# The first chunk's output projection turned round: weights standing, tokens moving

## The chip, the cores and the metric

The kernel runs on one core of one Trainium2 chip. The metric is the device time of one execution in microseconds (us). The kernel before took 358.76 us, the median of three runs (358.68 to 359.31 us).

## The reference

An attention-like scan is computed first; its result, laid out as 3072 tokens of 256 features, then goes through a gated feed-forward layer:

```python
def _attn_ref(x, a, B, C):            # x (4, 8, 768, 32); a (4, 8, 768); B, C (4, 8, 768, 16)
    log_a = np.log(np.clip(a, 1e-06, 1.0))
    for c in range(seq // 32):        # per batch and head
        cum = np.cumsum(la, axis=-1)
        L = np.exp(cum[:, :, :, None] - cum[:, :, None, :]) * causal
        y_intra = einsum('bhij,bhjd->bhid', einsum('bhin,bhjn->bhij', Cc, Bc) * L, xc)
        y_inter = einsum('bhin,bhnd->bhid', Cc, state) * exp(cum)[:, :, :, None]
        state = exp(sum(la)) * state + sum(Bx, axis=2)
    ...
def _moe_ref(x, w_gate, w_val, w_out):   # x (3072, 256); w (256, 1536), (256, 1536), (1536, 256)
    gate = 1.0 / (1.0 + np.exp(-(x @ w_gate)))
    val = x @ w_val
    return (gate * val @ w_out).astype(np.float32)
```

Everything is float32. The output is 3072 rows of 256 floats, 1 KB a row.

## The kernel before, in words

**Tiles and chunks.** The 768 positions of the sequence are cut into six chunks of 128. One chunk holds 128 positions of each of the four batches, so 512 tokens. For each chunk the scan gives the tokens' features, and then the feed-forward layer runs over twelve blocks `f` of 128 hidden features: TensorE (PE) makes a block's gate `pg` and value `pv` (128 features by 512 tokens, one PSUM bank each), ScalarE (ACT) takes the sigmoid of `pg` into `g`, and VectorE (DVE) multiplies it with `pv`, which gives the block `h`. When all twelve `h` of a chunk are there, the output projection `po` sums them against `w_out`.

**Two forms of a product.** Chunk 0's early products are plain float32 on whole weights (tiles `wr`, also `whole` in the code); a float32 matmul shows as two records on PE. Later products are made of a rounded high part and a low part in the type fp32r, three matmuls for one product (tiles `w`, `xh`, `xl`). All of chunk 0's `h` are single float32 tiles, and chunk 0's output projection is in plain float32 too.

**Two forms of the output projection.** `proj` (from L1190 in the code before, used by chunks 0 and 5) keeps 128 tokens of `h` standing in PE and moves 256 columns of the output weights: a tile of 128 tokens by 256 outputs for each batch. In chunk 0 that makes four accumulators of half a bank, 12 matmuls each (line L1214), a copy by ACT or DVE into a tile `o` (L1238) and one store of 128 rows of 1 KB (L1253). `proj_turned` (L1160 to L1192, used by chunks 1 to 4) keeps 128 columns of the weights standing and moves all 512 tokens of `h`: two accumulators of 128 outputs by 512 tokens, filled in turn by rounds of four blocks (L1176). DVE then turns them in squares of 32 by 32 (STREAM_TRANSPOSE, L1182) into a tile `o`, and 16 stores (L1189) each write 32 partitions, 32 KB, in pieces of 64 floats, 256 bytes.

**Order of the work.** The program is written out by a planner, `run()` (L194 to L283). Each piece of work is a task whose steps name an engine, a cost, what they need and what they make, and the buffers they take or give back. Among the steps that can begin, the planner takes the first by its model, with the lower due time first; a table `DUES` overrides due times by task name. What the planner writes is the fixed order of each engine's queue, and all five run in order. Three PSUM banks (`ps_mm`) go round between `pg`, `pv` and `po`; a bank comes free when ACT or DVE has read it. The scan's small matmuls (tiles `pcb`, `banks`, `local`) have banks of their own and stand on PE between the large ones, in insertions of about 16 to 64 small matmuls. They use decays that come by DMA from a DRAM tile `a_z` into six `ab` buffers (L341), are multiplied up by a scan on DVE (L484) and masked (L550, L686). All loads and stores after the start are issued by the queue SP in its own order: `tn`, `bn`, `xn`, `pp`, `ab` are inputs of the scan. Tiles of the tag `ut` (two buffers) hold the scan's result `y` of a pair of batches (L797) before it is split into `xh` and `xl`.

Of the kernel before, what the change touches and what calls it, by code (L numbers as in the profile page):

```python
# [15 lines left out]
DRAM = bass.MemoryType.DRAM  # L16

DUES = {
# [17 lines left out]
}  # L36
WARM = 3

# [35 lines left out]
def tile_ssd_then_gated_ffn(  # L74
# [11 lines left out]
    nc = tc.nc  # L86
# [574 lines left out]
    def faded(out, before, by, added, j):  # L661

        nc.vector.scalar_tensor_tensor(
            out=out[:, j], in0=before[:, j], scalar=by, in1=added[:, j], op0=ALU.mult, op1=ALU.add
        )
# [58 lines left out]
    class Pair:  # L724
# [44 lines left out]
        def after(self):  # L769

            p = self.p
            yield step("dve", 0.29, [("py", p)])
            pp = got["pp", p]
            local = [x.rearrange("p (j d) -> p j d", j=2) for x in fixed["local"]]
            ml = wk.tile([P, 2, NG * D], F32, tag="ml", name=f"ml{self.nm}")
            chosen(ml, local[0], 2)
            self.s1 = state_of(p, "sm")
            for j in range(2):
                yield step("dve", 0.42, [("pS", p - 2), ("ppp", p), ("pinter", p - 2)], [("pfirst", p)] if j else [], port=True)
                faded(self.s1, states2[p - 2], pp[:, j, L2 - 1 : L2], ml, j)  # L780
            if not self.more:
                return
            yield step("dve", 0.29, [], [("pafter", p)])
            mr = wk.tile([P, 2, NG * D], F32, tag="mr", name=f"mr{self.nm}")
            chosen(mr, local[1], 2)
            states2[p] = state_of(p, "sn")
            for j in range(2):
                yield step("dve", 0.42, [], [("pS", p)] if j else [], port=True)
                faded(states2[p], self.s1, pp[:, j, L - 1 : L], mr, j)

        def inner(self):

            p = self.p
            needs = [("whole", i) for i in range(NW)] if p == FIRST_P else [("plo", p - 2)]
            yield step("act", ACT_MM, [("py", p)] + needs, [("inner", p)])
            self.y = wk.tile([P, 2, NK, 2, L2], F32, tag="ut", name=f"y{self.nm}")
            nc.scalar.copy(self.y.rearrange("p i k u l -> p (i k) (u l)"), fixed["banks"][:, :, 2 * L : 3 * L])  # L797
# [242 lines left out]
    def halved(k, f):  # L1040
        return k == 0 and f < NHALF
# [113 lines left out]
    gs = {}  # L1155

    def turned(k):
        return 0 < k < NCH - 1

    outs = {}  # L1160

    def proj_turned(k, mt):

        ms = slice(mt * P, (mt + 1) * P)
        for n in range(0, NF, 4):
            some = range(n, n + 4)
            needs = [("h", k, f) for f in some] + sorted({("w", NF + f // 2) for f in some}) + ([] if n else [("gv", k)])
            yield step(
                "pe", 4 * 3 * 0.227, needs, [("proj", k)] if mt and n + 4 == NF else [], port=24, banks=int(n == 0)
            )  # L1170
            if n == 0:
                acc = ps_mm.tile([P, 512], F32, tag="mm", name=f"po{k}_{mt}")
            for f in some:
                w = wo[f // 2][:, f % 2, :, ms]
                for i, (part, of_h) in enumerate(((0, 0), (0, 1), (1, 0))):
                    nc.tensor.matmul(  # L1176
                        acc, w[:, part], hs[k, f][:, of_h], start=(f == 0 and i == 0), stop=(f == NF - 1 and i == 2)
                    )
        yield step("dve", 1.15, [("out", k - 2)], [("out", k, mt)], port=True, banks=-1)
        if mt == 0:  # L1180
            outs[k] = hp.tile([P, NB * RUN, 2 * 32], F32, tag=f"r{k % 2}", name=f"o{k}")
        nc.vector.transpose(outs[k].rearrange("p b (m t) -> p t b m", t=2)[:, mt], acc.rearrange("p (b r) -> p b r", r=32))  # L1182
        if mt == 0:
            return
        yield step("sp", 0.52 * 16, [("out", k, 0)], [("out", k)], 1.6)
        for b in range(NB):
            rows = out[b * S + k * L : b * S + (k + 1) * L].rearrange("(t r) m -> r t m", r=32)
            for q in range(NQ):
                nc.sync.dma_start(  # L1189
                    rows[:, :, 64 * q : 64 * q + 64], outs[k][32 * q : 32 * q + 32, RUN * b : RUN * b + RUN]  # L1190
                )

    def proj(k, j):
# [166 lines left out]
    def initial():  # L1360
# [2 lines left out]
        made = [(k, u) for k in keys for u in range(-6, 0)]  # L1363
        made += [(k, p) for k in ("plo", "pafter", "inner", "added") for p in range(2, FIRST_P)] + [("block", -1)]
        made += [("used", i) for i in (-2, -1)] + [(k, u) for k in ("cd", "inter") for u in range(2)]
        made += [("gv", -2), ("gv", -1), ("proj", -1), ("out", -1), ("out", 0)]
        yield step("none", 0.0, [], made)
        yield step("none", 4.9, [], [("a0",)])
        yield step("none", 0.6, [], [("bc", 0), ("bc", 1)])
# [145 lines left out]
```

## Time and profile before

The profiled execution took 358.8 us by its own time; its span, from the first to the last instruction, is 357.0 us.

| What | Before |
|---|---|
| Median of 3 runs | 358.76 us |
| Profiled execution: own time, span | 358.8 us, 357.0 us |
| PE busy | 349.7 us (98%), 3244 instructions |
| DVE, ACT, POOL busy | 164.0 us (46%), 148.3 us (42%), 167.8 us (47%) |
| Chunk 0's output matmuls (L1214) | 96 records |
| Granted PE clock | 1.00 in every stretch |

A row of a timeline reads: start in us, length in us, engine, line, operation, output <- inputs, shapes, number of instructions in the row, and in brackets what the engine waited for before it. The ends of matmuls are modelled and overlap, so the time that a stream of them takes is read from one start to the next. Group rows read: line, engine, operation, shapes, count | busy us, mean ns of one | idle before, and what ended it. SPq is the issuing of DMAs by the queue SP.

### The profile page before, as it was taken

What the parts mean: (1) busy time and instruction counts of PE and PEld (TensorE: products, weight loads), DVE (VectorE), ACT (ScalarE), POOL (GpSimd) and SP (SyncE); (2) the same over time, 40 slices, a digit from 0 to 9 for tenths busy, and PEclk for the clock granted to TensorE, in tenths of its full rate; (3) what the DMA queues carried; (4) which work ended last, traced back from release to release, by engine and by line L of the source; (5) the groups of instructions that cost most, each with busy time, mean ns of one, the idle gap of its engine ahead of it and who ended that gap; (6) DMA issues with size and microseconds to landing.
All of it is one profiled execution on the core that took longest, in us unless ns stands there. A gap on an engine that the chain in (4) does not pass through costs nothing.

```text
span 357.0 us, 7917 instructions
## 1 busy us (share of the span) xinstructions
PE 349.7 (98%) x3244; PEld 278.3 (78%) x3244; DVE 164.0 (46%) x287; ACT 148.3 (42%) x282; POOL 167.8 (47%) x171
## 2 busy tenths in 40 slices
PE   8989899999999999999999999999999999999996
PEld 3568378787788888888888888887888888888885
DVE  5879479877546684754650224530222210222201
ACT  2565984425885421355440244440044420344400
POOL 5536768666788635155460146562045520244400
PEclk9999999999999999999999999999999999999999
DMA  7989983515654345326320112000020000200000
GB/s 172 218 249 218 271 271 123 113 42 94 133 111 107 77 97 118 55 58 120 77 39 9 36 24 34 17 2 2 15 44 1 2 0 0 46 15 0 2 29 29
DMA packets 88949, 27.41 MB, mean 77 GB/s; under 512 B 78002, under 2 KB 81650, under 8 KB 88914
## 3 DMA queue, kind: packets, MB, share of 16 engines
q1 hardware_dynamic: 84754, 26.52, 31.6%
q10 hardware_dynamic: 4160, 0.39, 0.9%
q8 instruction: 25, 0.41, 0.5%
q14 instruction: 10, 0.08, 0.1%
HBM read 23.46 MB, written 3.44 MB: 75 GB/s over the span
## 4 chain that ended last, share of the span: by engine, by line
PE 88%; DMA 2%; ACT 2%; DVE 1%; SPq 1%; issue 0%
PE pg L1151 26%; PE pv L1151 25%; PE po L1176 18%; PE po L1214 6%; PE po L1225 2%; DMA wr<-in_moe_w_val_dram 2%; PE banks L693 2%; PE banks L677 1%; PE po L1226 1%; PE banks L719 1%; PE po L1222 1%; SPq L366 1%; PE pv L1142 1%; DVE wr L382 1%; PE local L700 0%; ACT wr L398 0%
## 5 line engine op out<-in xcount | busy, mean ns | idle before, releaser
L1119 POOL TENSOR_TENSOR h<-g,h 128x512 fp32r<-128x512 f32 x60 | 79.5, 1324 | 117.6 <-ACT h L1117 117.6
L1151 PE MATMUL pg<-xh,w 128*128 128x512 f32 x264 | 93.3, 394 | 0.0
L1151 PE MATMUL pv<-xh,w 128*128 128x512 f32 x264 | 92.2, 390 | 0.0
L1113 DVE TENSOR_TENSOR g<-pv,g 128x512 f32<-128x512 f32 x60 | 41.4, 691 | 91.1 <-PE pv L1151 89.6
L1117 ACT CAST h<-g 128x512 fp32r<-128x512 f32 x60 | 37.2, 620 | 73.1 <-DVE g L1113 73.1
L1176 PE MATMUL po<-h,w 128*128 128x512 f32 x288 | 66.7, 390 | 0.0
L1092 ACT ACTIVATE g<-pg 128x512 f32<-128x512 f32 x68 | 40.6, 597 | 55.9 <-PE pg L1151 55.2
L1176 PEld LDWEIGHTS po<-h,w 128*128 128x128 f32 x288 | 53.8, 188 | 11.3
L1151 PEld LDWEIGHTS pg<-xh,w 128*128 128x128 f32 x264 | 49.6, 188 | 11.1 <-issue 0.2
L1151 PEld LDWEIGHTS pv<-xh,w 128*128 128x128 f32 x264 | 49.6, 188 | 10.5 <-issue 0.2
L1151 PE MATMUL pg<-xl,w 128*128 128x512 f32 x132 | 51.4, 390 | 0.0
L1151 PE MATMUL pv<-xl,w 128*128 128x512 f32 x132 | 51.4, 389 | 0.0
L419 POOL TENSOR_TENSOR w<-wr,w 128x512 fp32r<-128x512 f32 x18 | 26.4, 1468 | 9.0 <-ACT w L417 9.0
L484 DVE TENSOR_TENSOR_SCAN ab<-ab,delta 128x512 f32<-128x512 f32 x20 | 28.5, 1437 | 1.6 <-DMA ab<-a_z 1.6
L1151 PEld LDWEIGHTS pg<-xl,w 128*128 128x128 f32 x132 | 24.8, 188 | 5.1 <-issue 0.2
L1151 PEld LDWEIGHTS pv<-xl,w 128*128 128x128 f32 x132 | 24.8, 188 | 5.1
L400 POOL TENSOR_TENSOR wr<-wr 128x512 int32<-128x512 int32 x18 | 21.9, 1224 | 13.5 <-ACT wr L398 7.4
L1182 DVE STREAM_TRANSPOSE o<-po 128x512 f32<-128x512 f32 x8 | 5.7, 717 | 41.8 <-PE po L1176 41.8
L1214 PE MATMUL po<-wr,h 128*128 128x256 f32 x96 | 23.2, 393 | 0.0
L1214 PEld LDWEIGHTS po<-wr,h 128*128 128x128 f32 x96 | 17.6, 188 | 3.8 <-issue 0.2
L820 POOL TENSOR_TENSOR xl<-y,xh 128x256 fp32r<-128x256 f32 x16 | 12.4, 775 | 10.8 <-ACT xh L818 10.6
L392 ACT ACTIVATE wt<-wr 128x512 f32<-128x512 f32 x18 | 12.0, 680 | 7.8 <-DVE wr L382 4.4
(145 smaller groups left out, 381.4 us busy)
## 6 DMA issues: line engine op xcount, KB each, us to landing
ab<-a_z SPq DMA_DIRECT2D x40, 128.0 KB
wr<-in_moe_w_gate_dram SPq DMA_DIRECT2D x6, 512.0 KB
wr<-in_moe_w_val_dram SPq DMA_DIRECT2D x6, 512.0 KB
wr<-in_moe_w_out_dram SPq DMA_DIRECT2D x6, 512.0 KB
xn<-in_x_dram SPq DMA_DIRECT2D x10, 256.0 KB
out_dram<-o SPq DMA_DIRECT2D x64, 32.0 KB
bn<-in_B_dram SPq DMA_DIRECT2D x10, 128.0 KB
tn<-in_B_dram SPq DMA_DIRECT2D x32, 32.0 KB
```

What stands on the lines that cost most here:

```text
L392: nc.scalar.activation(t, hw.bitcast(F32), AF.Prelu, scale=2.0**-112, alpha=2.0**32)
L400: nc.gpsimd.tensor_tensor(out=lw.bitcast(I32), in0=hw.bitcast(I32), in1=lw.bitcast(I32), op=ALU.add)
L419: engines[eng].tensor_tensor(out=lo, in0=lw, in1=hi.bitcast(F32), op=ALU.subtract)
L484: nc.vector.tensor_tensor_scan(out=t.rearrange("p h l -> p (h l)"), data0=t.rearrange("p h l -> p (h l)"), data1=delta.rearrange("p h l -> ...
L820: engines[eng].tensor_tensor(out=lo, in0=y, in1=hi.bitcast(F32), op=ALU.subtract)
L1092: nc.scalar.activation(gs[k, f], pm, AF.Sigmoid)
L1113: nc.vector.tensor_tensor(out=g, in0=pm, in1=g, op=ALU.mult)
L1117: copies[eng](hh, g)
L1119: engines[eng].tensor_tensor(out=hl, in0=g, in1=hh.bitcast(F32), op=ALU.subtract)
L1151: nc.tensor.matmul(pm, w[:, part, kt, fs], xx[:, kt], start=(i == 0), stop=(i == 3 * NK - 1))
L1176: nc.tensor.matmul(acc, w[:, part], hs[k, f][:, of_h], start=(f == 0 and i == 0), stop=(f == NF - 1 and i == 2))
L1214: nc.tensor.matmul(acc[:, :DM], hs[k, f][:, js], whole[NF + f // 2][:, f % 2], start=start, stop=stop, skip_group_check=True,)
```

## The change

Chunk 0's output takes the form of chunks 1 to 4. `turned(k)` is now true for chunk 0 as well, and `proj_turned` has a branch for single float32 blocks: a slice of the whole weights (every second column, 128 of them) stands, and the block's 512 tokens move. There are 24 matmuls of 128x512 (48 records) in place of 48 of 128x256 (96 records), and two accumulators in place of four. DVE turns each accumulator in two halves, into two tiles `o` of the tag `ut`, and SP issues 16 stores in 256 byte pieces in place of four stores of whole rows. Of the first pair of the scan in chunk 1, the step `inner`, which writes `y` into a `ut` tile, now needs chunk 0's output to be stored. The table `DUES` is replaced by another, which gives all engines a partly new order.

```diff
 DUES = {
-    "r": -31, "w6": -30, "w9": -25, "w11": 13, "w12": 14, "w13": 15, "w14": 16, "w15": 12.7, "w16": -2.4, "w17":
+    "r": -31, "w6": -30, "w9": -25, "w11": 8.5, "w12": 14.4, "w13": 269.7, "w14": 261.1, "w15": -0.5, "w16": -4,
...
         def inner(self):
             p = self.p
-            needs = [("whole", i) for i in range(NW)] if p == FIRST_P else [("plo", p - 2)]
+            needs = [("out", 0)] if p < FIRST_P + 2 else [("plo", p - 2)]
             yield step("act", ACT_MM, [("py", p)] + needs, [("inner", p)])
...
     def turned(k):
-        return 0 < k < NCH - 1
+        return k < NCH - 1
...
     def proj_turned(k, mt):
...
             for f in some:
+                if single(k, f):
+                    w = whole[NF + f // 2][:, f % 2].rearrange("p (m t) -> p t m", t=2)[:, mt]
+                    nc.tensor.matmul(acc, w, hs[k, f], start=(f == 0), stop=(f == NF - 1))
+                    continue
...
         yield step("dve", 1.15, [("out", k - 2)], [("out", k, mt)], port=True, banks=-1)
-        if mt == 0:
-            outs[k] = hp.tile([P, NB * RUN, 2 * 32], F32, tag=f"r{k % 2}", name=f"o{k}")
-        nc.vector.transpose(outs[k].rearrange("p b (m t) -> p t b m", t=2)[:, mt], acc.rearrange("p (b r) -> p b r", r=32))
+        n = 1 if k else 2
+        if mt == 0 and k:
+            outs[k] = [hp.tile([P, NB * RUN, 2 * 32], F32, tag=f"r{k % 2}", name=f"o{k}")]
+        elif mt == 0:
+            outs[k] = [wk.tile([P, NB * RUN // 2, 2 * 32], F32, tag="ut", name=f"o{k}_{i}") for i in range(2)]
+        for i in range(n):
+            nc.vector.transpose(
+                outs[k][i].rearrange("p b (m t) -> p t b m", t=2)[:, mt],
+                acc.rearrange("p (i b r) -> p i b r", i=n, r=32)[:, i],
+            )
         if mt == 0:
             return
         yield step("sp", 0.52 * 16, [("out", k, 0)], [("out", k)], 1.6)
...
                 nc.sync.dma_start(
-                    rows[:, :, 64 * q : 64 * q + 64], outs[k][32 * q : 32 * q + 32, RUN * b : RUN * b + RUN]
+                    rows[:, :, 64 * q : 64 * q + 64], outs[k][b * n // NB][32 * q : 32 * q + 32, at : at + RUN]
                 )
```

**On PE, the end of chunk 0's products.** `pv_11` is the last value block; `m`, `bd` and `xn` belong to an insertion of the scan of chunk 1, `cd`, `sn`, `sm` to the next. Before:

```order
L1151 MATMUL pv_11_803<-xh_425,w_738 128x512
L1214 MATMUL po_0_832<-wr_538,h_0_315 128x256
L1214 MATMUL po_0_832<-wr_538,h_1_354 128x256
L1214 MATMUL po_0_832<-wr_551,h_2_506 128x256
L1214 MATMUL po_0_832<-wr_551,h_3_540 128x256
L567 MATMUL pcb_1_687<-m_0_824,xn_0_297 32x64 x16
L578 MATMUL pcb_1_687<-xn_0_297,bd_0_839 32x64 x8
L567 MATMUL pcb_1_687<-m_1_830,xn_0_297 32x64 x16
L578 MATMUL pcb_1_687<-xn_0_297,bd_1_828 32x64 x8
L1214 MATMUL po_1_904<-wr_538,h_0_315 128x256
```

And now:

```order
L1152 MATMUL pv_11_804<-xh_425,w_735 128x512
L569 MATMUL pcb_1_628<-m_0_788,xn_0_297 32x64 x16
L580 MATMUL pcb_1_628<-xn_0_297,bd_0_829 32x64 x8
L569 MATMUL pcb_1_628<-m_1_826,xn_0_297 32x64 x16
L580 MATMUL pcb_1_628<-xn_0_297,bd_1_824 32x64 x8
L1179 MATMUL po_0_889<-h_0_315,wr_537 128x512
L1179 MATMUL po_0_889<-h_1_354,wr_537 128x512
L1179 MATMUL po_0_889<-h_2_505,wr_582 128x512
L1179 MATMUL po_0_889<-h_3_520,wr_582 128x512
L624 MATMUL pcb_1_628<-cd_833,sn_476 64x64 x4
```

The insertion stands directly behind the last value block instead of behind the first four output matmuls, and each output matmul moves 512 columns. Elsewhere on PE the insertions of the scan of chunks 2 and on stand behind other blocks than before; from the start of chunk 0's last products there are 17 insertions in both orders, with the same small matmuls.

**On DVE, at the end of chunk 0.** `o_0` and `o_1` are the two halves of the turned output, `g_0` is the first product of chunk 1's blocks, `m_0` and `m_1` are masks that the scan's insertion in chunk 1 needs. Now:

```order
L615 SCALAR_TENSOR_TENSOR sm_1068<-sn_512,pp_1_797,ml_2_1066 128x64
L1193 STREAM_TRANSPOSE o_0_1105<-po_0_889 128x256
L1193 STREAM_TRANSPOSE o_1_1106<-po_0_889 128x256
L641 TENSOR_TENSOR xl_937<-pcb_957,xh_936 128x2x2x64 x2
L588 TENSOR_TENSOR mr_2_1126<-pcb_957,mask 128x128
L518 SCALAR_TENSOR_TENSOR sn_1132<-sm_1068,pp_1_797,mr_2_1126 128x64
L688 TENSOR_TENSOR m_0_1164<-banks,ab_0_801 128x512
L1193 STREAM_TRANSPOSE o_0_1105<-po_1_930 128x256
L1193 STREAM_TRANSPOSE o_1_1106<-po_1_930 128x256
L688 TENSOR_TENSOR m_1_1180<-banks,ab_1_899 128x512
L1114 TENSOR_TENSOR g_0_1177<-pv_0_1170,g_0_1177 128x512
```

Before, no instruction on DVE read `po` of chunk 0; ACT copied the accumulators. The four transposes are new, two ahead of `xl` and two between `m_0` and `m_1`.

**On SP, at the start of chunk 1.** Now all 16 stores of chunk 0 stand in one piece ahead of the loads `pp_0`, `bn_1`, `ab_1`, `pp_1`, `tn_0` and `ab_2` (of the eight rows of `tn_0` two are shown):

```order
L343 DMA ab_0_1134<-a_z 64x512 x2
L308 DMA bn_0_1162<-in_B_dram 128x16x16
L1204 DMA out_dram<-o_0_1105 32x4x64 x8
L1204 DMA out_dram<-o_1_1106 32x4x64 x8
L354 DMA pp_0_1275<-a_q 128x1x128 x2
L308 DMA bn_1_1288<-in_B_dram 128x16x16
L343 DMA ab_1_1291<-a_z 64x512 x2
L354 DMA pp_1_1317<-a_q 128x1x128 x2
L321 DMA tn_0_1331<-in_B_dram 32x4x64
L321 DMA tn_0_1331<-in_C_dram 32x4x64
...
L343 DMA ab_2_1433<-a_z 64x512 x2
```

Before, the stores of the four batches stood in two pairs, the second of them here:

```order
L341 DMA ab_0_1201<-a_z 64x512 x2
L1253 DMA out_dram<-o_2_1084 128x256
L1253 DMA out_dram<-o_3_1155 128x256
L352 DMA pp_0_1227<-a_q 128x1x128 x2
L319 DMA tn_0_1245<-in_B_dram 32x4x64
L319 DMA tn_0_1245<-in_C_dram 32x4x64
```

So 16 store issues now stand where two stood. On DVE the scan of `ab_2` stands between the products `g_6` and `g_7` of chunk 1, and it waits for that load.

More of the change, by code (lines that the diff above doesn't have):

```diff
@@ L772, in after @@
             yield step("dve", 0.29, [("py", p)])
-            pp = got["pp", p]
             local = [x.rearrange("p (j d) -> p j d", j=2) for x in fixed["local"]]
@@ L779, in after @@
                 yield step("dve", 0.42, [("pS", p - 2), ("ppp", p), ("pinter", p - 2)], [("pfirst", p)] if j else [], port=True)
-                faded(self.s1, states2[p - 2], pp[:, j, L2 - 1 : L2], ml, j)
+                faded(self.s1, states2[p - 2], got["pp", p][:, j, L2 - 1 : L2], ml, j)
             if not self.more:
@@ L788, in after @@
                 yield step("dve", 0.42, [], [("pS", p)] if j else [], port=True)
-                faded(states2[p], self.s1, pp[:, j, L - 1 : L], mr, j)
+                faded(states2[p], self.s1, got["pp", p][:, j, L - 1 : L], mr, j)
         def inner(self):
             p = self.p
-            needs = [("whole", i) for i in range(NW)] if p == FIRST_P else [("plo", p - 2)]
+            needs = [("out", 0)] if p < FIRST_P + 2 else [("plo", p - 2)]
             yield step("act", ACT_MM, [("py", p)] + needs, [("inner", p)])
@@ L1166, in proj_turned @@
             some = range(n, n + 4)
-            needs = [("h", k, f) for f in some] + sorted({("w", NF + f // 2) for f in some}) + ([] if n else [("gv", k)])
+            needs = [n for f in some for n in ([("h", k, f, i) for i in range(2)] if halved(k, f) else [("h", k, f)])]
+            needs += sorted({("whole" if single(k, f) else "w", NF + f // 2) for f in some}) + ([] if n else [("gv", k)])
             yield step(
-                "pe", 4 * 3 * 0.227, needs, [("proj", k)] if mt and n + 4 == NF else [], port=24, banks=int(n == 0)
+                "pe", sum(0.88 if single(k, f) else 0.681 for f in some), needs,
+                [("proj", k)] if mt and n + 4 == NF else [], port=24, banks=int(n == 0)
             )
@@ L1188, in proj_turned @@
             for q in range(NQ):
+                at = RUN * (b % (NB // n))
                 nc.sync.dma_start(
-                    rows[:, :, 64 * q : 64 * q + 64], outs[k][32 * q : 32 * q + 32, RUN * b : RUN * b + RUN]
+                    rows[:, :, 64 * q : 64 * q + 64], outs[k][b * n // NB][32 * q : 32 * q + 32, at : at + RUN]
                 )
@@ L1365, in initial @@
         made += [("used", i) for i in (-2, -1)] + [(k, u) for k in ("cd", "inter") for u in range(2)]
-        made += [("gv", -2), ("gv", -1), ("proj", -1), ("out", -1), ("out", 0)]
+        made += [("gv", -2), ("gv", -1), ("proj", -1), ("out", -2), ("out", -1)]
         yield step("none", 0.0, [], made)
```

34 rows, old and new, of the table DUES are left out of this document.

## The prediction

> **What bounds the kernel now.** I read the page first: busy shares and the chain that ended last.
>
> ```profile
> PE 349.7 (98%) x3244; PEld 278.3 (78%) x3244; DVE 164.0 (46%) x287; ACT 148.3 (42%) x282; POOL 167.8 (47%) x171
> PE 88%; DMA 2%; ACT 2%; DVE 1%; SPq 1%; issue 0%
> ```
>
> TensorE is busy 98% of the span, and 88% of the chain is its own work. Shares are means, so I cut the span at the edges of the stages in the view of busy time by windows (length, then busy us and count of PE, PEld, DVE, ACT, POOL, then the clock, DMA share, GB/s):
>
> ```profile
> 0.00:42.20 42.20, 38.02 (x398) 23.41 (x398) 29.43 (x61) 24.68 (x53) 21.72 (x35) 1.00 0.90 218
> 42.20:61.50 19.30, 19.28 (x111) 14.96 (x112) 15.57 (x20) 13.94 (x28) 14.69 (x14) 1.00 0.68 219
> 61.50:89.03 27.53, 27.53 (x417) 21.51 (x415) 21.34 (x33) 11.92 (x30) 18.36 (x22) 1.00 0.41 86
> 89.03:353.90 264.87, 264.87 (x2328) 218.40 (x2320) 97.18 (x173) 97.74 (x172) 113.01 (x103) 1.00 0.21 43
> 353.90:357.00 3.10, 0.05 (x1) 0.00 (x0) 0.42 (x1) 0.00 (x0) 0.00 (x0) 1.00 0.25 85
> ```
>
> The granted clock is full throughout. In the first 42.2 us loads matter (DMA engines 90% busy) and PE waits 4 us. From 42.2 to 353.9 its busy time is the length of the window, so it never waits; 3.1 us of last stores follow. Chunk 0's output stands in the third window. Three things can move the time: the start of PE's closed stretch, the sum of PE's work in it, or a new wait that opens it. A gain on any other engine is worth nothing there.
>
> **The start.** Up to 42 us the queues of all engines stand as before, but for two value blocks and a gate block exchanged on PE and one small DVE step; the chain into the value block that ends the waiting is unchanged. I take zero, with 0.3 us either way: half of the last wait before it.
>
> ```profile
> 42.22 1.99 PE L1142 MATMUL pv<-xw,wr 128*128 128x512 f32 x4 [0.61 <-ACT g L1092]
> ```
>
> **PE's work removed.** The stream of the old output matmuls, from PE's timeline and from its group:
>
> ```profile
> 67.13 3.89 PE L1214 MATMUL po<-wr,h 128*128 128x256 f32 x16
> 71.58 7.52 PE L1214 MATMUL po<-wr,h 128*128 128x256 f32 x32
> L1214 PE MATMUL po<-wr,h 128*128 128x256 f32 x96 | 23.2, 393 | 0.0
> L1214 PEld LDWEIGHTS po<-wr,h 128*128 128x128 f32 x96 | 17.6, 188 | 3.8 <-issue 0.2
> ```
>
> Sixteen more records take 7.52 - 3.89 = 3.63 us, 0.227 us a record (the 393 ns of the group is a pipelined length and overlaps the next). 96 x 0.227 = 21.8 us go.
>
> **PE's work added.** 48 records of 512 columns in float32. The same shape, type and 128x128 weights stand in the trace at the early gates and values:
>
> ```profile
> 34.65 1.88 PE L1142 MATMUL pg<-xw,wr 128*128 128x512 f32 x4
> 38.08 1.88 PE L1142 MATMUL pg<-xw,wr 128*128 128x512 f32 x4
> 26.56 1.03 PE L1048 MATMUL pg<-xw,wr 128*128 128x256 f32 x4
> 27.42 1.03 PE L1048 MATMUL pv<-xw,wr 128*128 128x256 f32 x4
> L1142 PEld LDWEIGHTS pg<-xw,wr 128*128 128x128 f32 x8 | 1.6, 196 | 1.4 <-issue 1.4
> ```
>
> Between the two rows at 34.65 and 38.08 stands one more of four, so eight records take 3.43 us, 0.429 each: 48 x 0.429 = 20.6 us, a gain of 1.2 us. Where does it come from? Columns are the same in number. At 256 columns L1048 took 0.86 us for four, 0.215 a record, half of 0.429; L1214 took 0.227 at the same size and type. So the old output matmuls carry about 12 ns a record that the early ones do not. One difference in the code is the moving operand: L1214 moves whole weights with every second word left out, L1048 and L1142 move contiguous tokens. The new matmul moves a contiguous `h`; its strided operand is the weights, as at L1142, whose loads took 196 ns for 188 and hide under 429.
>
> Bounds. If the 12 ns belong to every record of this stage, whatever moves, the new one takes 0.441 and the gain is 21.8 - 21.2 = 0.6 us. If time goes by columns at the old rate, 2 x 0.227 = 0.454 and the gain is zero. Above that no row points: a load would have to last over twice its 196 ns to show. I take 0.429, since this is the nearest row in shape, type and operands, and keep 0 to 1.2.
>
> The page "TensorE: Matmul & The Clock Gate" of the Trainium skill (section "Back-to-back issue gap") gives the isolated gap as columns by 2.4 GHz plus 2.5 ns, which says that halving the count of matmuls saves 2.5 ns each. An estimate from it is 48 x 2.5 = 0.12 us, no gain that can be seen. The early rows (215 and 429 ns, against its estimates of 216 and 429 for two columns' cycles each) agree; the 227 of L1214 does not.
>
> **Insertions.** Both orders hold 17 insertions of the scan between large matmuls in the closed stretch, with the same small matmuls, so I cost their moves at nothing on PE. What makes their inputs is hidden beside PE, with margins: the first, now directly behind `pv_11`, needs two masks.
>
> ```profile
> 59.83 0.67 DVE L550 TENSOR_TENSOR m<-pcb,ab 128x512 f32<-128x512 f32 x1
> 61.01 0.68 DVE L550 TENSOR_TENSOR m<-pcb,ab 128x512 f32<-128x512 f32 x1
> 61.50 1.97 PE L1214 MATMUL po<-wr,h 128*128 128x256 f32 x8
> ```
>
> The second ended at 61.69 before, and is now one product earlier in DVE's queue. `pv_11` ends at 61.5 and the second mask's matmuls come some 0.4 us later. If that cover is gone, PE waits 0.3 us or less.
>
> **ACT, DVE.** ACT loses four copies of 366 ns, which PE never waited for. DVE gains four transposes of 128x256:
>
> ```profile
> L1238 ACT COPY o<-po 128x256 f32<-128x256 f32 x4 | 1.5, 366 | 8.3 <-PE po L1214 8.3
> L1182 DVE STREAM_TRANSPOSE o<-po 128x512 f32<-128x512 f32 x8 | 5.7, 717 | 41.8 <-PE po L1176 41.8
> L811 DVE TENSOR_TENSOR y<-banks,y 128x256 f32<-128x256 f32 x8 | 3.4, 423 | 10.3 <-ACT y L797 4.5 <-PE local L719 4.3 <-PE banks L700 1.5
> 89.21 1.29 DVE L686 TENSOR_TENSOR m<-banks,ab 128x512 f32<-128x512 f32 x2 [0.87 <-PE banks L677]
> ```
>
> Half of 717 ns is 359, another PSUM read of that size took 423; I take 0.42, 1.7 us in all, between 1.4 and 2.9 (each as dear as a whole one). DVE is 21.3 of 27.5 us busy there. Behind the last two wait `m_1` and `g_0`: `po` ends about 87.1 (the insertion behind it takes 0.7), `m_0` begins 0.2 behind the insertion, 0.65 of the two in the last row, and is done at 88.7, so the transposes end at 89.6, and `m_1` and `g_0` at about 91.0; its bank is wanted by the third block after it, past 92. Cost nothing; at the upper price half a microsecond.
>
> **SP.** Sixteen store issues replace four and now stand ahead of loads that chunk 1 needs. The rows that price them:
>
> ```profile
> 146.11 9.98 SPq L1189 DMA_DIRECT2D out_dram<-o  x16
> 200.05 7.57 SPq L1189 DMA_DIRECT2D out_dram<-o  x16
> 93.98 0.40 SPq L319 DMA_DIRECT2D tn<-in_B_dram  x1
> 98.18 0.43 SPq L319 DMA_DIRECT2D tn<-in_C_dram  x1
> 98.66 1.21 SPq L352 DMA_DIRECT2D pp<-a_q  x2
> 99.92 2.00 SPq L341 DMA_DIRECT2D ab<-a_z  x2
> 102.03 0.53 SPq L306 DMA_DIRECT2D bn<-in_B_dram  x1
> 163.76 1.12 SPq L341 DMA_DIRECT2D ab<-a_z  x2
> 167.85 1.23 DVE L484 TENSOR_TENSOR_SCAN ab<-ab,delta 128x512 f32<-128x512 f32 x1 [0.19 <-DMA ab<-a_z]
> L1113 DVE TENSOR_TENSOR g<-pv,g 128x512 f32<-128x512 f32 x60 | 41.4, 691 | 91.1 <-PE pv L1151 89.6
> 116.59 0.28 DVE L663 SCALAR_TENSOR_TENSOR sm<-sq,pp,ml 128x64 f32<-128x64 f32 x1
> 58.77 0.39 PE L1151 MATMUL pg<-xh,w 128*128 128x512 f32 x1
> 60.13 0.39 PE L1151 MATMUL pv<-xh,w 128*128 128x512 f32 x1
> 94.74 0.69 PE L677 MATMUL banks<-bct 32*64 32x128 f32 x32
> 96.54 0.50 PE L1151 MATMUL pg<-xh,w 128*128 128x512 f32 x1
> ```
>
> The stores can begin at 89.6 and take 7.6 to 10.0 us of issuing: until 97.2 to 99.6. Then `pp_0` 1.2, `bn_1` 0.5, `ab_1` 1.1 to 2.0, `pp_1` 1.2, eight of `tn_0` 4.6, `ab_2` 1.1 to 2.0, and about 0.1 between them, 0.5: the issue of `ab_2` ends at 107.4 to 111.6. An `ab` was there 2.97 us after its issue ended (164.88 to 167.85): 110.4 to 114.6. The scan (1.23), a small step (0.28) and `g_7` (0.69) follow on DVE, which gives back a bank at 112.6 to 116.8. PE wants it for `pg_9`. Its start: `pg_0` at 87.9 (89.03 less the 1.2), 18 blocks of 1.36 (58.77 to 60.13), and one insertion of 2.0 (94.74 to 96.54, and the slower first record after it): 114.4. So at the fast end there is a margin of 1.8 us, at the slow end a wait of 2.4. I take the fast end, no wait: the rows of 0.43 us are the many, the slow ones single. `ab_1`, due before `g_5`, comes by the same sum 3 us after 100.3 to 103.6; its scan, a small step, a mask and `g_5` then end at 106.2 to 109.5, for a bank that `pg_7` wants at 109.0 (14 blocks and the insertion): it binds less.
>
> **The sum.** The profiled execution took 358.8 us, 357.0 of span and 1.8 around it; its time and the median of the runs (358.76) are one. 358.8 - 1.2 = 357.6 us.
>
> **The rivals.** A measurement of this kernel can tell about 0.2%, 0.7 us, from no change: under 358.04 is faster, over 359.48 slower.
>
> *The extra 12 ns stay.* For it: the fp32r records (58.77 to 60.13 is six) also start every 0.227 us, 12 ns over half of 0.429, though they move no strided operand. Against: L1142 and L1048. Then 358.8 - 0.6 = 358.2. Chance 0.14.
>
> *Columns alone count*, 0.454 a record: 358.8. Against it stands L1214 beside L1048: the excess was not there at the same columns. Chance 0.07. The rule of the Trainium skill's page "TensorE: Matmul & The Clock Gate" comes out beside it: 358.8 less the estimate of 0.12 is 358.7.
>
> *SP's stores delay `ab_2`.* One mechanism: sixteen issues hold back six groups of loads, DVE stands in its scan of `ab_2`, `g_7` behind it keeps a bank, PE stops ahead of `pg_9`. It decides from 1.8 us of delay over the fast sum, so from stores that take 9.4 us with all else fast. Up to a wait of 1.9 us the gain is only eaten: 357.6 to 359.5, chance 0.15. At the slow end, 357.6 + 2.4 = 360.0, slower; so too if the stores take 12 us with fast loads (4.4 us late, 2.6 of wait: 360.2). For it: one of two rows has 9.98. Against: in that stretch the 0.43 us issues are the many and the long ones single. Chance 0.15.
>
> *Another wait from the new order* that eats the gain, in chunks 2 to 5, where all insertions have moved: 0.04, with the time at 358.8.
>
> **How the numbers follow.** The forecast, 357.6, has 0.45; with the start's 0.3 either way it stretches from 357.2 to 357.9. Faster: 0.45 and a small part, 0.05, of the mild delay and the staying 12 ns: 0.50. Slower: 0.15. Same: 0.35. The range leaves out the dear end of the SP case and a gain beyond 1.7: 357.1 to 359.5, which takes in both ends of the matmul's price and a wait of up to 1.9 us.
>
> **What would show it.** Right: 48 records at the new line, four of them every 1.72 us in a stretch without insertions; `pg_0` of chunk 1 starting near 87.9; busy time equal to length from 42.2 to about 352.7; no wait in front of `pg_9`; the issue of 16 stores under 9 us. The first rival shows as 1.76 us for four, the second as 1.82. The SP case shows as idle PE near 114, released by DVE's `g`, with DVE released by the DMA of `ab`. I am wrong beyond size if PE's first closed stretch begins elsewhere than at 42.2, or if PE's idle time after it is over 1 us.

## The result

The changed kernel takes 362.41 us, the median of six runs (361.45 to 365.08). The kernel before, timed beside it, takes 358.84 us (358.41 to 359.31). The ratio is 1.0116, with an interval of 1.0087 to 1.0144: slower by 1.2%, where a gain of 1.2 us was forecast. The time lies outside the predicted range.

The profiled execution took 361.84 us by its own time, with a span of 360.0, so it stands 0.6 us under the median. From the page of the changed kernel, busy shares and the chain that ended last:

```profile
span 360.0 us, 7831 instructions
PE 350.4 (97%) x3196; PEld 275.3 (76%) x3196; DVE 165.0 (46%) x291; ACT 146.5 (41%) x281; POOL 165.8 (46%) x168
PE 85%; DMA 3%; DVE 3%; issue 3%; ACT 3%; SPq 2%; DVEq 0%; ACTq 0%
```

PE has 48 records fewer and yet is busy 0.7 us longer, and "issue" went from 0% to 3% of the chain. The windows cut at the same stages as in the prediction (columns as there):

```profile
0.00:41.88 41.88, 37.87 (x399) 23.45 (x399) 28.41 (x61) 24.68 (x53) 22.03 (x35) 1.00 0.92 209
41.88:61.59 19.71, 19.71 (x111) 14.69 (x111) 14.76 (x20) 13.91 (x28) 13.94 (x13) 1.00 0.72 236
61.59:88.53 26.94, 26.94 (x369) 18.51 (x368) 18.12 (x32) 10.90 (x25) 16.25 (x18) 1.00 0.46 91
88.53:356.70 268.17, 265.86 (x2328) 218.64 (x2320) 103.30 (x177) 96.99 (x176) 113.55 (x104) 1.00 0.21 42
356.70:360.00 3.30, 0.00 (x1) 0.00 (x0) 0.42 (x1) 0.00 (x0) 0.00 (x0) 1.00 0.23 79
```

The third window, in which chunk 0's output stands, is shorter by 0.6 us (26.94 for 27.53). The fourth is longer by 3.3 (268.17 for 264.87): same number of PE records, but 2.3 us in which PE is idle, where it had no idle time at all. The tail, from PE's last record to the end of the span, is 0.25 longer (3.28 for 3.03; the last window before still holds 0.05 us of PE's work). What PE waited for from 42.5 us on, in the view of waits (total, times, longest):

```profile
PE banks L702 <- issue: 2.0, 2, 1.8
PE pv L1143 <- ACT g L1093: 0.6, 1, 0.6
PE pg L1152 <- DVE g L1114: 0.3, 1, 0.3
```

The middle row was there before. The last is the wait ahead of `pg_9` that the prediction's SP rival named. The first is the large one, and its releaser is "issue": PE waited for nothing that the profile shows. Its two places in PE's timeline:

```profile
134.23 0.22 PE L702 MATMUL banks<-xn,bd 64*32 64x64 f32 x1
136.28 0.30 PE L702 MATMUL banks<-xn,bd 64*32 64x64 f32 x2 [1.83 <-issue]
136.51 0.50 PE L1183 MATMUL po<-h,w 128*128 128x512 f32 x1
...
184.26 0.34 PE L702 MATMUL local<-xn,bd 64*32 64x64 f32 x6
184.77 0.25 PE L702 MATMUL banks<-xn,bd 64*32 64x64 f32 x2 [0.16 <-issue]
```

At 134.23 PE stops with two small matmuls (four instructions with their loads) of an insertion still to do, and goes on 2.05 us later. Their operands had long been there, since others of the same line had just used them, and neither the load nor the matmul at which PE goes on has a semaphore to wait for. A later insertion stops in the same way at 184.5.

**What they share.** The page's table of DMA queues has, in both kernels, a queue that brings instructions:

```profile
q8 instruction: 25, 0.41, 0.5%
```

25 transfers make 0.41 MB, 16 KB each. I numbered PE's instructions in the trace, loads, matmuls and the few others, from the start. There are 6429 of them, so 257 to a transfer. Both stops stand in front of a number that leaves 193 when divided by 256 (3009 and 4289). The count can be had from windows that end at the two stops (the bracket behind PE and the one behind PEld):

```profile
0.00:135.50 135.50, 130.12 (x1490) 93.55 (x1490) 92.94 (x158) 75.56 (x153) 86.17 (x94) 1.00 0.64 151
135.50:184.60 49.10, 48.32 (x638) 39.44 (x639) 31.03 (x56) 19.13 (x37) 23.15 (x25) 1.00 0.44 85
```

638 + 639 and 3 other instructions of PE that these columns leave out make 1280, five times 256, between the two stops. So a block edge of PE's code stands there. PE passes such edges all the time without a trace; these two have in common that another edge stands in the same insertion, 256 instructions ahead. An insertion with all its parts holds 320 instructions (160 small matmuls with their loads, more than the 16 to 64 named in the description of the kernel) and takes 2.26 us, about 7 ns each, while large matmuls take 113 ns an instruction (0.227 us for a load and a matmul). In an insertion with two edges PE uses up a whole block in under 2 us. In the changed kernel the edges moved, since 96 instructions were gone ahead of them and the insertions stand behind other blocks. In the kernel before, one insertion after 42 us holds two edges as well, the one at 150.70 us (at its 10th and 266th instruction), and PE passes both without a stop. So two edges in one insertion are not the whole condition; experiment 2 takes this up.

The sum of the difference in span, 3.0 us: pauses 2.28 + 0.39 (the insertions took 4.54 and 2.65 us for 2.26), the wait ahead of `pg_9` 0.48 (its idle time and a slower entry), other small differences in chunks 1 to 4 0.1, tail 0.25, chunk 0's output -0.6, and up to it +0.1 net (start 0.34 earlier, the stretch to 61.59 0.43 longer, for which I have no cause).

### The profile page after: what moved, and what is told of

The parts are those of the page before. It is cut to its first block, busy times and chain, and to the rows that moved or that the text cites. A ratio compares the mean times of both kernels' runs of the same rounds, so it can differ in the third digit from the quotient of the medians.

```text
span 360.0 us, 7831 instructions
## 1 busy us (share of the span) xinstructions
PE 350.4 (97%) x3196; PEld 275.3 (76%) x3196; DVE 165.0 (46%) x291; ACT 146.5 (41%) x281; POOL 165.8 (46%) x168
## 4 chain that ended last, share of the span: by engine, by line
PE 85%; DMA 3%; DVE 3%; issue 3%; ACT 3%; SPq 2%; DVEq 0%; ACTq 0%
PE pg L1152 22%; PE pv L1152 22%; PE po L1183 18%; PE po L1179 6%; PE po L1240 2%; DMA wr<-in_moe_w_val_dram 2%; PE banks L695 1%; PE warm L135 1%; PE banks L679 1%; PE po L1241 1%; DMA ab<-a_z 1%; SPq L321 1%; PE pg L1049 1%; PE banks L721 1%; DVE ab L486 1%
## 5 line engine op out<-in xcount | busy, mean ns | idle before, releaser
L486 DVE TENSOR_TENSOR_SCAN ab<-ab,delta 128x512 f32<-128x512 f32 x20 | 29.3, 1474 | 2.5 <-DMA ab<-a_z 1.6
L1193 DVE STREAM_TRANSPOSE o<-po 128x512 f32<-128x512 f32 (+1 forms) x12 | 7.3, 621 | 44.4 <-PE po L1183 42.3
L402 POOL TENSOR_TENSOR wr<-wr 128x512 int32<-128x512 int32 x18 | 20.2, 1128 | 13.5 <-ACT wr L400 9.8
L821 POOL TENSOR_TENSOR xl<-y,xh 128x256 fp32r<-128x256 f32 x16 | 13.4, 845 | 26.3 <-ACT xh L819 19.5
L1179 PE MATMUL po<-h,wr 128*128 128x512 f32 x48 | 22.5, 616 | 0.0
L1179 PEld LDWEIGHTS po<-h,wr 128*128 128x128 f32 x48 | 14.4, 311 | 5.1 <-issue 0.2
```

The source lines that it names most:

```text
L402: nc.gpsimd.tensor_tensor(out=lw.bitcast(I32), in0=hw.bitcast(I32), in1=lw.bitcast(I32), op=ALU.add)
L486: nc.vector.tensor_tensor_scan(out=t.rearrange("p h l -> p (h l)"), data0=t.rearrange("p h l -> p (h l)"), data1=delta.rearrange("p h l -> ...
L821: engines[eng].tensor_tensor(out=lo, in0=y, in1=hi.bitcast(F32), op=ALU.subtract)
L1179: nc.tensor.matmul(acc, w, hs[k, f], start=(f == 0), stop=(f == NF - 1))
```

## The experiments

In the expectations, C is the theory just told (code: two block edges in one insertion), and D that data are the cause: chunk 0's 16 stores, by what they hold back or fill. W says that the strided weight load keeps half of the matmul gain; K, that a pause can also make the clock fall. Each kernel was timed beside the kernel before on the same chip, and ratios go by that.

**1. Shift the code.** 64 more instructions on PE at 70.8 us (32 small loads and 32 records of small matmuls), in both kernels: the step `multiply_after` does its products twice. This costs PE 0.5 us and moves every later block edge by 64 instructions against the insertions.

```diff
         multiply(pcb, 0, *(units[u] for u in then))
+        multiply(pcb, 0, *(units[u] for u in then))
```

In the changed kernel this leaves no insertion with two edges, in the kernel before it makes two others of them, and the one at 150.70 has one edge left.

> The changed kernel with 16 of the scan's small matmuls written twice (the same values into the same place, in the insertion at 70.8 us, in the middle of chunk 0's output). That puts 64 more instructions (32 weight loads, 32 matmul records) into TensorE's stream there and costs about 0.45 us; nothing else moves. Theory C (code): the pauses in the insertions at 134.2 and 184.4 us are TensorE waiting for its next block of 256 instructions, because two block edges fall into one insertion of 320 instructions; shifted by 64, no insertion holds two edges with the request for the second inside it. Both pauses (about 2.0 and 0.4 us) are gone and the time is 359.6 to 360.2. Theory D (data): the pauses are waits for loads that stand behind the 16 stores; they stay, and the time is 362.3 to 362.9.

> The kernel before with the same 64 extra instructions in the same insertion (at 70.9 us there), 0.45 us. Theory C: counted from the same block edges, the edges in the insertion at 121.3 us move from instruction 98 to 34 of 320, so a second one falls into it: a pause of 0.7 to 2.2 us there, perhaps 0.7 more in the one at 215.5; 360.0 to 362.1. Theory D: only the 0.45, 359.2.

The changed kernel with more work became faster: 360.1 us (359.97 to 361.01), ratio to before 1.0039 (1.0026 to 1.0052), in place of 1.0116. The kernel before became 363.38 us (362.79 to 363.97), ratio 1.0122 (1.0103 to 1.0141): 4.4 us for 0.5 us of work. Waits of the shifted changed kernel from 42 us on:

```profile
PE pt L464 <- ACT bct L473: 1.0, 1, 1.0
PE pv L1144 <- ACT g L1094: 0.6, 1, 0.6
```

"issue" is gone (the first row is the last wait of the start, just inside the window). Of the shifted kernel before, the waits that are new (the 0.6 us for `g` stands in it too) and their places:

```profile
PE banks L701 <- issue: 1.2, 1, 1.2
PE local L701 <- issue: 1.1, 1, 1.1
```

```profile
125.39 0.33 PE L701 MATMUL banks<-xn,bd 64*32 64x64 f32 x5
126.82 0.24 PE L701 MATMUL local<-xn,bd 64*32 64x64 f32 x2 [1.10 <-issue]
...
221.33 0.23 PE L701 MATMUL local<-xn,bd 64*32 64x64 f32 x2
222.72 0.30 PE L701 MATMUL banks<-xn,bd 64*32 64x64 f32 x4 [1.16 <-issue]
```

Two pauses have come up in just the two insertions that now hold two edges, +1.41 and +1.39 us, at numbers 2753 and 4801: 193 again, 2048 apart. This kernel has neither the turned output nor its stores. So the shift takes pauses away and makes them, as C said. The expectation for the time of this kernel was too low, 360.0 to 362.1, since the clock was not in it: in this profile it fell besides to 0.55 at 42.3 to 46.0 us, behind waits of PE at the start (a window; the third number from the end is the clock), and the stage from 42.36 us to the first output matmul takes 20.86 us for 19.28 before.

```profile
42.30:46.00 3.70, 3.64 (x5) 1.69 (x6) 0.69 (x1) 2.95 (x8) 3.70 (x4) 0.55 1.00 352
```

**2. Shift it further.** 160 more instructions in the changed kernel instead of 64, at the same place.

```diff
         multiply(pcb, 0, *(units[u] for u in then))
+        multiply(pcb, 0, *(units[u] for u in then))
+        multiply(pcb, 0, *(units[u] for u in then))
+        multiply(pcb, 0, units[then[0]])
```

> The changed kernel with the small matmuls of that insertion written two and a half times more, 160 more instructions, about 1.1 us. Theory C: the pause moves: none at 135 and 185, one of 0.7 to 2.2 us in the insertion at about 122.4 (its edges at 38 and 294 of 320); 361.0 to 362.5. Theory D: the pause stays in the insertion at about 135; 363.

360.52 us (360.17 to 361.05), ratio 1.0043 (1.0026 to 1.006). Its waits from 42 us on:

```profile
PE pv L1146 <- ACT g L1096: 0.6, 1, 0.6
PE pg L1155 <- DVE g L1117: 0.3, 1, 0.3
```

Both old pauses are gone. But the insertion at 122.6 us holds two edges now, at its 38th and 294th instruction, and took 2.15 us: the pause that C expected there did not come, and the time lies under its 361.0 to 362.5. So two edges are not enough. The DMA records of the instruction queue give the reason. For all thirteen insertions after 42 us with two edges in the profiles (us; names are those of the experiments, "changed again" is a later profile of the changed kernel):

```
kernel                 insertion   fetch of the block     PE passes      from fetch end   pause
                       begins      behind the 2nd edge    the 2nd edge   to that
changed                131.97      134.08 to 135.00       136.28         1.28             2.28
changed                182.52      182.07 to 183.38       184.77         1.39             0.39
half the stores        130.95      133.06 to 134.10       135.46         1.36             2.47
half the stores        181.73      181.78 to 182.70       184.03         1.33             0.44
changed again (1)      131.52      133.64 to 134.65       136.08         1.43             2.52
changed again (1)      183.96      183.76 to 185.20       186.64         1.44             0.82
changed again (2)      131.96      134.15 to 135.10       136.52         1.42             2.64
changed again (2)      184.30      184.02 to 184.94       186.37         1.43             0.22
before, shifted by 64  123.52      124.19 to 125.55       126.82         1.27             1.41
before, shifted by 64  219.30      220.35 to 221.46       222.72         1.26             1.39
only the due times     172.16      173.08 to 174.31       175.68         1.37             1.63
changed, by 160        122.63      121.75 to 122.79       124.44         1.65             none
before                 150.70      148.40 to 149.62       152.48         2.86             none
```

In eleven of them PE goes on 1.26 to 1.44 us after the fetch of the block ended, whatever the pause; in the last two the fetch had begun 0.88 and 2.30 us ahead of the insertion, was there 1.65 and 2.86 us before the edge, and nothing waited. Counted in the same way for all 264 edges behind the first ones in the eleven profiles, none is passed sooner than 1.26 us after its fetch ended. So PE waits for its next block of code, and a block can be used some 1.3 us after its transfer. What sets the start of a fetch (from 2.3 us before the insertion to 2.2 behind its start) is not settled: the later the first edge in the insertion, the later the fetch as a rule, but the insertion at 122.63, with its first edge at the 38th instruction, breaks it.

**3. Take half the data away.** Eight of chunk 0's 16 stores are left out (so the second half of the features of chunk 0's output isn't written).

```diff
-            for q in range(NQ):
+            for q in range(NQ if k else NQ // 2):
```

> The changed kernel with 8 of the 16 stores of chunk 0 left out (half of that chunk's output isn't written), so that SP is free some 3.8 us sooner at 93.7. The wait of 0.3 us at 115.3, where TensorE waits for a product on VectorE that stands behind the scan of the late decays, should go: 0.3 to 0.5 us less. Theory C: the pause at 134 stays, 361.3 to 362. Theory D: the loads come sooner and the pause at 134 shrinks or goes, 359.5 to 360.5.

361.59 us (360.88 to 365.53), ratio 1.0088 (1.0053 to 1.0124). Its waits:

```profile
PE banks L702 <- issue: 2.3, 2, 2.1
```

The wait for `g` ahead of `pg_9` is gone, so that one does come from the stores. The pauses stay, at the same instruction numbers, and the time is the one that C expected. D falls as the cause of the pauses.

**4. The strided load.** On top of the first shift, chunk 0's output weights are taken as 128 columns that follow each other instead of every second one (each still two words from the next, as in the early gates; so chunk 0's output columns come out in another order).

```diff
-                    w = whole[NF + f // 2][:, f % 2].rearrange("p (m t) -> p t m", t=2)[:, mt]
+                    w = whole[NF + f // 2][:, f % 2, ms]
```

> The changed kernel with the 64 extra instructions (which took the pauses away: 360.1 us), and in chunk 0's output the standing weights are 128 neighbouring columns in place of every second one (chunk 0's output columns come out in another order; nothing else moves). Theory W (weight load): the first matmul after each of the five insertions in the middle of chunk 0's output waits for its weights, and the strided load takes 311 ns for 188 to 196; with neighbouring columns the first spacing falls from 0.655 to about 0.53 us, so 0.6 us less in all: 359.5. Theory R (record): a record of 512 float32 columns itself starts dearer behind an insertion; the first spacing stays 0.65 and the time 360.1.

359.34 us (358.64 to 360.33), ratio to before 1.0012 (0.9994 to 1.003): 0.8 us under the same kernel with every second column (timed on another chip; the intervals of the two ratios overlap, so the spacings below decide). The load's group in the changed kernel, then in this one:

```profile
L1179 PE MATMUL po<-h,wr 128*128 128x512 f32 x48 | 22.5, 616 | 0.0
L1179 PEld LDWEIGHTS po<-h,wr 128*128 128x128 f32 x48 | 14.4, 311 | 5.1 <-issue 0.2
```

```profile
L1180 PEld LDWEIGHTS po<-h,wr 128*128 128x128 f32 x48 | 9.0, 196 | 9.3 <-issue 8.8 <-POOL cd L508 0.2
66.64 3.71 PE L1180 MATMUL po<-h,wr 128*128 128x512 f32 x8
70.28 1.21 PE L538 MATMUL pcb<-bct 32*64 32x128 f32 x64
```

And the same eight records in the changed kernel:

```profile
67.09 3.82 PE L1179 MATMUL po<-h,wr 128*128 128x512 f32 x8
70.84 0.69 PE L538 MATMUL pcb<-bct 32*64 32x128 f32 x32
71.47 7.26 PE L1179 MATMUL po<-h,wr 128*128 128x512 f32 x16
```

Eight records take 3.75 us with every second column (67.09 to 70.84) and 3.64 with columns that follow each other. In the steady stream the load hides: (7.26 - 3.82) / 8 = 0.43 a record, as forecast. But behind each insertion the first load has nothing to hide under that lasts long enough, and 311 ns for 196 show as 0.11 us. W is confirmed; the price is paid at each of the insertions among these matmuls.

**5. One half of the change alone.** First the turned output with the due times of before, then the old output with the new due times (only the table is exchanged; the first, against the changed kernel, and the second, against the one before, with the two lines the other way round):

```diff
 DUES = {
-    "r": -31, "w6": -30, "w9": -25, "w11": 8.5, "w12": 14.4, "w13": 269.7, "w14": 261.1, "w15": -0.5, "w16": -4,
+    "r": -31, "w6": -30, "w9": -25, "w11": 13, "w12": 14, "w13": 15, "w14": 16, "w15": 12.7, "w16": -2.4, "w17":
...
```

> The changed kernel's turned output with the due times of before, so that the planner makes another order; no insertion of 320 instructions in it has a block edge between its 25th and its 70th instruction. Theory C (the loss of the changed kernel lies in where its new order puts the insertions against the block edges): no pause inside an insertion, the gain of 0.6 us of chunk 0's output stays: 358.3. Rival S (the 16 stores on SP, or another cost of the turned output itself, take the gain back whatever the order): 359 to 360.

> The kernel before, chunk 0's output as it was, with the due times of the change, planned anew. The edge stands at the 32nd instruction of the insertion in the middle of chunk 2's blocks. Theory C: one pause of 0.4 to 1.4 us there, and 0.25 us more at the very end of the program, where the changed kernel's order of the last tiles ends later in all its runs: 359.5 to 360.7. Rival S: the due times alone cost nothing, 358.9 to 359.2.

Turned output alone: 360.7 us (359.85 to 361.43), ratio 1.0053 (1.0037 to 1.007). The expected 358.3 was missed. No insertion has two edges and PE never waits for "issue", but a new wait stands at the first block of chunk 1:

```profile
87.21 0.29 PE L622 MATMUL pcb<-cd,sm 32*64 32x64 f32 x8
88.86 0.49 PE L1150 MATMUL pg<-xh,w 128*128 128x512 f32 x1 [1.35 <-ACT xh L636]
```

Here the insertion whose result becomes chunk 1's `xh` stands directly ahead of `pg_0`, so that the block has to wait until ACT has read it. In the full change chunk 0's last output matmuls stand between the two. So each half of the change needs the other: this wait is what the turned output costs in the old order. With 0.25 us at the end of the program it makes 1.6 of the 2.4 us over the expected time; the rest is not traced.

New due times alone: 365.69 us (364.63 to 367.95), ratio 1.0208 (1.0159 to 1.0257), over the expected 359.5 to 360.7. Its waits from 42.5 us on:

```profile
PE pg L1153 <- ACT xh L638: 1.8, 1, 1.8
PE banks L702 <- issue: 1.3, 1, 1.3
PE po L1216 <- POOL wr L402: 0.9, 1, 0.9
...
PE pv L1153 <- ACT g L1094: 0.5, 1, 0.5
```

The second row is C's pause, in the one insertion that holds two edges; the other rows are waits that the expectation did not see. The table fits its own code alone. The tail of this kernel is 3.03 us, as before, while that of the turned output alone is 3.29 (3.28 in the changed kernel): the 0.25 us at the end belong to the turned output and not to the due times. Why, I did not find.

**6. The clock.** Three of the six executions of the changed kernel had a mean granted clock of 0.99 to 0.995, and these are the longest (362.66, 364.28, 365.08; the others, at 1.00, take 361.45 to 362.16). The first profile was one of the latter. So the changed kernel was profiled twice more.

> The changed kernel once more, for one profile. Three of its six executions had a mean granted clock of 0.99 to 0.995 and took 1 to 3 us more. Theory K: a pause of about 2 us inside the closed stretch can let the granted clock of TensorE fall, and the matmuls behind it then start 0.45 us apart in place of 0.227 for some 3 us; in a profile with such a mean clock the slow stretch stands behind 136 or 185 us, and costs about 1.7 us. Rival B: the fall stands at about 42 us, behind the two waits there (in one profile of the kernel before with the extra instructions it did: 0.55 from 42.3 to 46.0), and has nothing to do with the change. Where the mean clock is 1.00 this run tells nothing on that; the pause at 134 us is then seen again, 1.5 to 2.5 us.

> The same kernel a second time, with the same expectations: theory K, a slow stretch behind 136 or 185 us; rival B, one behind 42 us; with a mean clock of 1.00 neither, and a pause of 1.5 to 2.5 us at 134.

363.7 and 363.41 us, both with a mean clock of 0.995 (before beside them: one execution, 359.89, at 0.995 too). Windows around the pause in the first, the third number from the end being the granted clock:

```profile
133.00:137.00 4.00, 1.91 (x76) 1.54 (x66) 0.59 (x2) 0.07 (x1) 0.41 (x1) 1.00 0.30 80
137.00:141.00 4.00, 4.00 (x13) 3.12 (x12) 3.46 (x10) 1.22 (x3) 2.68 (x3) 0.58 0.82 105
141.00:150.00 9.00, 9.00 (x100) 7.30 (x98) 4.18 (x7) 0.91 (x2) 0.65 (x2) 1.00 0.54 115
```

And in the second:

```profile
133.00:137.00 4.00, 1.91 (x102) 1.52 (x97) 0.03 (x1) 0.00 (x0) 0.41 (x1) 0.90 0.38 99
137.00:141.00 4.00, 4.00 (x13) 3.15 (x14) 3.49 (x9) 1.30 (x3) 2.11 (x3) 0.68 0.72 96
```

Just behind the pause the clock is 0.58 and 0.68 over 4 us; PE runs 13 records there where 17 or 18 fit (4 / 0.227). In both, the trace's record of the clock is 0.50 for one stretch of 3.41 us, from 137.65 us in the first and from 136.18 in the second. At full clock the first would have saved 4 x 0.42 = 1.7 us. So the fall stands where K said, and a pause of 2 us can cost nearly as much again. It need not: the first profile has the same pause and no fall. Over all timed executions with a recorded clock, 13 of 24 of the kernels with pauses had a mean of at most 0.996, and 6 of 63 of those without. In the profile of the shifted kernel before, the fall stood behind waits at the start, so not every low mean comes from a pause of this kind.

## Why the prediction was wrong

*What bounds it, the start:* right. PE's closed stretch begins at 41.88 for 42.22, 0.34 us earlier where 0.3 was allowed; it moved from 41.4 to 42.8 between the profiles, so this difference says nothing.

*The sign of error:* the prediction called itself wrong beyond size if PE's idle time behind the start were over 1 us. It was 2.3 us.

*Insertions:* this is the step that failed. "With the same small matmuls, so I cost their moves at nothing on PE" is true of their work (2.26 us for a full insertion wherever nothing disturbs it), but their place against the blocks of PE's code changed, and that costs 2.7 us in the profiled execution and, with the clock, about 3 more in the longest execution. The case "another wait from the new order" had a chance of 0.04; this is where the time went, though in no way that a look at data and buffers could have shown. The counts were in reach: the trace before shows 256 instructions to a block and 320 in an insertion. They would have raised the doubt without pricing it, since the insertion at 150.70 us there holds two edges and doesn't stop.

*The matmuls:* the mechanism was right and the size wrong. A record takes 0.43 us in the steady stream, as taken from the early gates. Chunk 0's output matmuls took 22.19 us of PE for 22.81, a gain of 0.6 and not 1.2. The step that was mis-sized is the bound on the load: "a load would have to last over twice its 196 ns to show". The prediction took the new weights to stand as at L1142; they stand twice as far apart, since every second of the two-word elements is taken. The load lasts 311 ns, and though that is under 429, it shows behind each insertion, where the load has only a small matmul to hide under. The 0.6 is also the figure of the rival of the extra 12 ns, but not by its reason: that rival wanted 1.76 us for four records in the steady stream, and they take 1.72.

*ACT, DVE:* right. The transposes take 426 ns, the estimate was 0.42, and nobody waits for them:

```profile
L1193 DVE STREAM_TRANSPOSE o<-po 128x256 f32<-128x256 f32 x4 | 1.6, 426 | 2.1 <-PE po L1179 2.1
```

*SP:* the forecast was no wait; there was a small one, by a term that was taken too short. The stores and what follows, rows of the timelines of SP, POOL, DVE and PE in order of time:

```profile
89.79 7.76 SPq L1204 DMA_DIRECT2D out_dram<-o  x16
106.28 2.21 SPq L343 DMA_DIRECT2D ab<-a_z  x2
...
111.17 2.57 POOL L1120 TENSOR_TENSOR h<-g,h 128x512 fp32r<-128x512 f32 x2
111.57 3.26 DVE L486 TENSOR_TENSOR_SCAN ab<-ab,delta 128x512 f32<-128x512 f32 x1 [0.87 <-DMA ab<-a_z]
...
114.93 0.68 DVE L1114 TENSOR_TENSOR g<-pv,g 128x512 f32<-128x512 f32 x1
115.66 0.50 PE L1152 MATMUL pg<-xh,w 128*128 128x512 f32 x1 [0.32 <-DVE g L1114]
```

The stores begin where the sum put them and take 7.76 us, the fast end. `ab_2` lands at 111.57, 1.2 after the fast sum. The 1.8 us of margin would have covered that. But the scan takes 3.26 us for the 1.23 put in, and two products of POOL, 2.57 us, run beside it from 111.17 on; so `g_7` comes at 114.93 and PE is 0.32 us idle. The rival's chain of events happened, with the delay in another link.

*The sum:* 358.8 - 0.6 + 2.7 (pauses) + 0.5 (`pg_9`) + 0.25 (tail), with 0.2 of small differences, gives 361.85, the profiled 361.84. The first two experiments settle what PE waits for in the pauses. An estimate without them is 359.2 (the profiled 361.84 less 2.67) to 359.6 (the shifted kernel's 360.1 less the 0.5 of the extra instructions; its wait at `pg_9` is gone too), still no gain. With the weights of experiment 4 the third window came out 1.2 us ahead of before, the extra instructions set aside, as forecast; their 0.5 us, the wait at `pg_9`, the tail and small waits gave it back, and the kernel stood level with before. None of the versions tried beats the kernel before.

## What to carry to other kernels

Where a kernel holds dense bursts of small instructions, count them: if a burst uses up a whole block of code (256 instructions here) faster than the next can be brought, its place against the block edges and the start of the fetch count, and any edit ahead of it, even the removal of work, can make or cure a stall that no wait explains. A pure shift by a few harmless instructions tests it at once, and separates what an edit does from where it puts the rest. And a load or a wait that hides in a steady stream must be priced again at every place where the stream starts anew.

## What the runs showed of the hardware

PE's code comes in blocks of 16 KB. The Trainium skill's page "Runtime: NRT & Kernel Launch" (section "Instruction fetch mechanics") says the same, and that the next block is fetched while the present one runs, so that the fetch is mostly hidden. The trace agrees on size and number, and after 42 us on the hiding for every edge but eleven of the thirteen in the table above. In such an insertion a block of 256 is used up in about 1.8 us, less than the fetch (0.9 to 1.5 us) and the 1.3 us behind it together, so the fetch is hidden only where it begins early enough, as in the last two rows.

The granted clock fell to half for 3.41 us after idle times of 2.1 us. The Trainium skill's page "TensorE: Matmul & The Clock Gate" (section "Why this matters for your kernels") asks for no idle gaps over about 3 us; the rows of experiment 6 show 0.58 and 0.68 over 4 us behind shorter ones, though not in every execution.

A weight load of 128x128 in float32 took 188 to 196 ns in this kernel's other gate, value and output products, and 311 ns where its columns stand twice as far apart as in the early gates. A DVE scan that takes 1.22 us by the median took 3.26 beside POOL's products on tiles of the same size. The other profiles show the pattern: 75 scans of this shape took over 1.3 us, each began while a TENSOR_TENSOR of POOL was running, and all but this one ended 1.08 to 1.09 us after that instruction did. This one saw out 0.92 us of one product and the 1.32 of the next. The 71 scans beside which POOL had nothing running took at most 1.23 us. So the scan seems to wait for POOL's instruction to end, though some that began beside one took 1.2 us all the same; no run tried it by itself.
